# Two taps per matmul in the short convolution of the last 64 channels, plain loads on two issuing queues, and a new table of work

## The chip, the cores and the metric

The kernel runs on one core of a Trainium2 chip. The metric is the time of one execution on the device in microseconds (us); lower is better. TensorE (PE) multiplies matrices, VectorE (DVE), ScalarE (ACT) and GpSimd (POOL) do elementwise work, and SyncE (SP) does nothing but issue transfers. The transfers themselves (DMA) are moved by 16 DMA engines. Each of the five engines runs its own list of instructions in order.

## The reference

Two independent blocks are computed, and their outputs stand side by side in the last dimension (576 + 576 columns, 2048 rows, bf16).

Block A is an attention over four segments of 512 rows with 32 heads of 18 dimensions. Each segment has causal softmax attention of its own, plus a read of a memory that the earlier segments have summed up; a gate mixes the two, and a projection follows:

```python
for s in range(4):
    p = softmax(qs @ ks.T * scale + mask)           # 512 x 512 for each of 32 heads
    a_dot = p @ vs
    a_mem = (phi(qs) @ M) / (phi(qs) @ z + 1e-6)    # phi(t) = t+1 for t>0, else exp(t)
    outs.append(g * a_mem + (1 - g) * a_dot)
    M = M + phi(ks).T @ vs; z = z + phi(ks).sum(rows)
out_A = concat(outs) @ wo
```

Block B works on 576 channels of length 2048. The part that the change touches is the first line, a causal convolution with four taps for each channel:

```python
k_shift[s, c] = sum(shift_k[c, i] * k[s - i, c] for i in range(4))
kv = k_shift * v
y  = long_convolution(kv, ssm_k) + kv * ssm_D       # by a Fourier transform of length 4096
out_B = q * y
```

## The kernel before

The program is first recorded as a graph of about 1,600 small pieces of work (`Graph.add`), each with a name, the engines that may run it, and the tiles that it reads and writes. The order in which they are then written out is not decided by the code: it is a table, `ORDER`, of three characters for each piece (two for its number, one for its engine), and a second table, `PLACES`, says which copy of a tile each buffer gets. `place` reads both. So an engine's list of instructions follows the table, and a piece that has to wait holds up all that stands behind it in the same engine's list. Loads and stores are pieces too. In the kernel before all of them are on SP, and there are 225 of them. The semaphores of the DMAs go round eight places: each transfer waits at its issue until the transfer eight before it in the program has landed.

**Block A.** For each segment `s`, x is loaded transposed (`x{s}.{t}`, tiles `xT`), q and k are multiplied out in five groups of heads (`qk{s}.{m}`, tiles `dn`), written to a scratch in memory (`qd`, L861, `qk_scratch`) and read back padded to 32 rows a head (`pad`, L871). Four heads at a time (`i` from 0 to 31) the scores are computed (L1046), put through exp on ScalarE (`exs0_i`, `exs1_i`, `exs2_i`, L1053), masked on GpSimd (L1060) and multiplied with V (`av{i}`). The result goes by `ou` to a second scratch (`ad`, L1141, `a_scratch`), is read back in another layout (`am`, L1186, and the sums of the softmax as `cs`, L1156), normalised and mixed, and multiplied by `wo` (`out{s}.{tt}`, evacuated to one of two `oA` tiles by `eout`, stored by `oA{s}.{tt}`, L1255).

**Block B.** The channels are cut into groups of 128, 128, 128, 128 and 64. For each group k and v are loaded transposed, channels on partitions (`kT{ct}`, L374, and `vT{ct}`, L377, tiles `X4`, called `X` in the profile). The last group has only 64 new channels, and it loads the 128 channels from 448 on and uses the upper half. `conv` does the short convolution on TensorE: for each tap a diagonal 128 x 128 matrix of that tap's weights (`dg`, L388) times the transposed k, shifted by one column more for each tap, all four summed in PSUM. For each group there are four blocks of 512 columns, so 16 matmuls of 512 columns a group. `kv` (L404) multiplies by v. The rest of block B is a two-stage Fourier transform as matmuls (`F1`, `F2`), a product in frequency (`Q`, `P`, `Yi`, `Yr`), the way back (`inv`), a transposing transfer (`zt`, L566), a last stage and the product with q.

**Start of the program.** The tables of the transform are made on the chip: `w1idx` (DVE), `w1sin` (ACT, L258), `w1mask` (POOL), `psie` (POOL), and with these `psiT`, the first piece of work on TensorE; then four sines of 1024 columns (`sin`, L295) from index tiles that DVE makes (`idx`, L288 and L290). The loads at the start, in the order of SP's list: `wv`, five `x0` (L800), the rest of `wv`, `wk`, `beta1`, the rest of `wk`, the taps (`sk4`, L362, and `sk`, L357), `wq`, the first `kT0` and `vT0`, `Dt` (the 576 values of ssm_D as 4 partitions by 144, L350), the scratch's zeros.

Of the kernel before, what the change touches and what calls it, by code (L numbers as in the profile page):

```python
# [122 lines left out]
class Prog:  # L123
# [47 lines left out]
    def dma(self, name, fn, r, w, prio, nb, pk=1024, eng=16, issue=0.6, lat=1.5, al=()):  # L171
        per = {64: 0.009, 128: 0.012, 256: 0.018, 512: 0.028, 576: 0.030, 1024: 0.048, 1152: 0.052, 2048: 0.088, 4096: 0.160}
        k = min(per, key=lambda x: abs(x - pk))
        work = nb / pk * per[k] / eng
        return self.g.add(name, {"SP": issue}, fn, r=r, w=w, prio=prio, lat=lat, work=work * self.p["dmaw"], al=al)
# [52 lines left out]
    def build_b_front(self):  # L228
# [117 lines left out]
        def ld2(e):  # L346
            d = self.t(self.Dt)[:]
            dst = bass.AP(d.tensor, d.offset, [[32 * d.ap[0][0], 4], [1, 144]])
            src = bass.AP(self.B_D.tensor, self.B_D.offset, [[1, 4], [4, 144], [1, 1]])
            self.nc.sync.dma_start(out=dst, in_=src)  # L350

        g.add("Dt0", {"POOL": 0.3}, lambda e: self.nc.gpsimd.memset(self.t(self.Dt)[:, 0:144], 0.0), w=[self.Dt], prio=PT)
        self.dma("Dt", ld2, [], [self.Dt], p["prio_cl"], 1152, pk=64)

        def ld3(e):
            t = self.t(skb)
            self.nc.sync.dma_start(out=t[:, 0:4, :], in_=self.B_sk[0:512, :].rearrange("(t p) f -> p t f", p=P))  # L357
        self.dma("sk", ld3, [], [(skb, 0)], p["prio_cl"], 4096, pk=64)

        def ld4(e):  # L360
            t = self.t(skb)
            self.nc.sync.dma_start(out=t[:, 4, :], in_=self.B_sk[448:576, :])  # L362
        self.dma("sk4", ld4, [], [(skb, 1)], p["prio_cl"], 1024, pk=64)

    def conv(self, ct):
# [6 lines left out]

        def lk(e, kT=kT, c0=c0):
            self.nc.sync.dma_start_transpose(out=self.t(kT)[:, 16:16 + S], in_=self.B_k[0, :, c0:c0 + P])  # L374

# [3 lines left out]
        o = self.dma("kT%d" % ct, lk, [], [(kT, 1)], pr - p["lead_kt"], S * 256, pk=4096, issue=3.5, lat=1.8)  # L379
# [5 lines left out]
        def dgf(e, kT=kT, dg=dg, ct=ct):  # L385
            v = self.nc.vector if e == "DVE" else self.nc.gpsimd
            v.memset(self.t(kT)[:, 0:16], 0.0)
# [4 lines left out]
        for c in range(4):  # L392
            pc = Buf("ps1", "psconv")

            def cm(e, pc=pc, c=c, kT=kT, dg=dg):
                o = self.psf(pc)
                for i in range(4):
                    self.mm(o, self.t(dg)[:, i, :], self.t(kT)[:, 16 + 512 * c - i:16 + 512 * c - i + 512], i == 0, i == 3)
# [206 lines left out]
    def build_a_consts(self):  # L605
# [3 lines left out]
        for nm, src, lead in (("wq", "A_wq", 0), ("wk", "A_wk", 0.1), ("wv", "A_wv", 4), ("wo", "A_wo", 40)):  # L609
# [3 lines left out]
            if nm != "wo":  # L613
# [5 lines left out]
                def l1(e, b=b, src=src):  # L619
                    self.nc.sync.dma_start(out=self.t(b)[:, 0:4, :], in_=getattr(self, src)[0:512, :].rearrange("(t p) f -> p t f", p=P))  # L620

                def l2(e, b=b, src=src):
                    self.nc.sync.dma_start(out=self.t(b)[64:128, 4, :], in_=getattr(self, src)[512:576, :])

                self.dma(nm, l1, [], [(b, 0)], pr, 512 * 1152, pk=1152)
                self.dma(nm + "4", l2, [], [(b, 1)], pr, 64 * 1152, pk=1152)
            else:
                def l1(e, b=b):
                    self.nc.sync.dma_start(out=self.t(b)[0:126, 0:4, :], in_=self.A_wo[0:504, :].rearrange("(t p) f -> p t f", p=126))

                def l2(e, b=b):
                    self.nc.sync.dma_start(out=self.t(b)[0:72, 4, :], in_=self.A_wo[504:576, :])

                self.dma(nm, l1, [], [(b, 0)], pr, 504 * 1152, pk=1152)
                self.dma(nm + "4", l2, [], [(b, 1)], pr, 72 * 1152, pk=1152)
# [8 lines left out]
        def lb(e):  # L644
            src = bass.AP(self.A_beta.tensor, self.A_beta.offset, [[1, 32], [0, 4], [1, 1]])
            self.nc.sync.dma_start(out=self.t(bt)[:, 0:1], in_=src)

        self.dma("beta", lb, [], [(bt, 0)], p["prio_w"] + 20, 256, pk=64)

        for h in range(2):  # L650
            def lb2(e, h=h):
                src = bass.AP(self.A_beta.tensor, self.A_beta.offset + 16 * h, [[1, 16], [0, 8], [1, 1]])
                self.nc.sync.dma_start(out=self.t(bt)[:, 1 + h:2 + h], in_=src)

            self.dma("beta%d" % h, lb2, [], [(bt, 1 + h)], p["prio_w"] + 20, 256, pk=64)

        def lb3(e):
            src = bass.AP(self.A_beta.tensor, self.A_beta.offset + 28, [[0, P], [1, 4]])
            self.nc.sync.dma_start(out=self.t(bt)[:, 3:7], in_=src)

        self.dma("beta2", lb3, [], [(bt, 3)], p["prio_w"] + 20, 1024, pk=64)
# [80 lines left out]
        for j in range(4):  # L742
            def lw(e, j=j):
                self.nc.sync.dma_start(out=self.t(self.wop)[32 * j:32 * j + DH, :], in_=self.A_wo[504 + DH * j:504 + DH * j + DH, :])

            self.dma("wop%d" % j, lw, [(self.wop, "z")], [(self.wop, j)], self.tA(16), DH * 1152, pk=1152)
# [524 lines left out]
SHAPES = dict(A=([P, 4096], "bf16"), q=([P, 2048], "bf16"), xs=([P, 2048], "bf16"), X4=([P, 2064], "bf16"), H=([P, 1024], "bf16"), X=([P, 1024], "bf16"), T=([P, 1024], "bf16"), dg=([P, 4, P], "bf16"), xT=([P, L], "bf16"),  # L1271
# [14 lines left out]
    "0YG00G01D0oG02G0pD03D0cS0+S0-S11S10S0bG0qG06G04A05G0VG0RG0GG0HP07D08A0ID09D0BG0wG0zS0dS0ZS0iS0aS0US0XS0WS0TS1MG1RG0vG"  # L1286
    "0AA0CD0tSGoS0jSGpS0hS26P1wP22P14P18P1xA0DA19AGqD27D23D0ED1lD1CP12P1AP1kA13A1DD15D0FA1iGGrPGxPGvPGtP0rS0gSGWS1mD2BS0SS"
    "1BD0yS1YS0xSGyDGsDGwDGuD16P1nA0kA0PP0LP0NP17A1yP0QA0OAGzD1hA1zA0MDGXD1UP1VD0nG1oD1pDIiGH6PGaPGcPH4PGkPHAPG+PGdDGlDHCP"
    "GbAH7AHBAH5AHDAGiPGjD1XSIgS2CS0uSH2PGmPH0PH8PGYPGgPIOS1bSGnD1jD2AS1cSH1AG-A28P1NPH3A29AH9DGePHKPHXPI1PHIPHJDHLDGZAICS"
    "IDS1WS0sS1SP24PHYDGfAGhA1OA0lD20PI2A1TA25AHZPHxPHEPHkPHGPHTPHaAHyDH-PHzPHFDHlDI0AHHDHMD1GPH+AHNDI3D1PP1HAHUAIPD1qA1rD"  # L1290
    "HPG1KP1QA1LA1uD1sDHVPHWAI4DHbGI5DI6DHmPHOGHdGHnA1tA1EPHcG2QP1FA2RA1IP1+P2SA1-AIQPIWPISP21D1JDIXDIRAIUPIcPIePIdD0JPIVA"
    "IfAITAHoP0KD2XPHiPIaP2YA2ZAHpDHjDHQPIYP2IPIbD1vDIZDHRAHSA1ZS2KA2JAHeDHqDHrDHsDIpPIjPHtD2MP2NA2OA4cS4aS4bS4dS4ZS2PG2LG"
    "2aGJ6P4ePIhSJ7D5fP4fD5DD5gA2bP2dAJcP4iP2cA5CA4jA5IA2ES1eSKGS2DS4gP2TGIkDIqDJdD2qPHfP4hD5JD5EDHhD2UP2VDHgD1aS1dS4yS2WS"
    "0fSInPIoD2rA2sA59AKHD5KDJpP2iPJqA0mG5AG2jAIlP2kA4kP4lAKaG2eG2tG5GGImDIrD5BD2xPJrPHuPHwDHvD4mP2zA5FA2yAI7P4nAI8AI9DJsD"
    "5PGIwPIyPJNPJ0PIsPJ2PIxDJ4P5HDJ3DIuPIvDJ5D2lG2+GIzAItAJOAJ1AJ8P5OAJ9AJLP2fPI+P4oP5QD4pDI-AJCPJvPJtPJMA2gA2mPJDAJwAJuD"
    "JxDJyD5MD5dPIBS2FPIAS2GD2HD2oA2nAJeP2-P5eAIGP2pG2hSIIPIJDKYSJfA30A31A32GKUPJAPKMPKOPKSP64S65SIHDIKPJzGKPDKVAKNAKZS4+S"
    "KQPJPPKWPKIPJRPILDJBAJ+GKTAJSAJQDJgPJaPIEPKJDJbD5LA5NDIFDKRAKXA4sP4tA5RAJhD5SD5TDJEDJFDJTGJUDIMSJHDINS4zS1gSJWG4qP4rA"
    "2uP66S2vA33P34A3AP3BAJVG67SJGG2wS40S35S1fSK5S3wSK4SKbPKdP3CA5UAKcD5VDKeD5WD3EP3GAKfPKhP3FA3DG36P3HG37A38A39GKgDKiDKjD"
    "KKP4uPKLAJXP3LPLFP4vAJiGJjGJkGJYAJlGJZDLGDKwPKsPKqPKoP5bDKrD3NA3MAK+PKyP3IPKkPL0PKpDK-DKzDKlDKxAKtA5aA3JAL1A5cD4wP3PP"
    "4xD50S43S3KS3OGMSGKuPKvD54S51SJIP3QA3RAJKD3aPKmPJmP3xDKnD5YD3bA3cAJ-PL2PJoDJnAJJDL3AL4PLDP3WP3SG3yG5XAK1AL5D3TPK0D5ZD"  # L1300
    "K3S3UD3VSK2S3dGL6G46SMQSLJPLKD41P44P42D45D3YA3XA68S3ePLUPLEA3gA3fA3hGLVDL7DLjPLkD3ZG3lP3mA3nAL9G3oG5tP3pP5uDLWP3rA3qA"
    "3iPLYPLXD5vDLnPLoDLZA3sG6GP6HA6IA62P3jDLHPK8PLSPKAP63DLTA3tP3kSK9DKBD3uA6CP6DA52S6EALIA3vS5hP5wPMRS5lP5jPLaDLbD5nP5kA"
    "5iD5xD5oD5mAKCPK6P6JGLLG6KPKDD3zSK7DL8DLMD3+D0eS49S4CS5rP5pPMTP60P5qD61D53S6LA8dS8fS8hS8eS8gS5sA6MA3-G6RPMXPMUDMYDMZP"
    "47P6TA6SA6VPKFSM8SKES4-S6XA6WA6FG6UG55S6NGLdG6YG69P48DMaD6AD5+P4DPMVP6gP4ED5yP4AP6hA6iAMWD5-D4BD6BD5zD6OP6ZP6PA6cP4FP"
    "4KP8iP6aA6eA6dAMbD6jGLNG4MP4HP6bS58S6QS4LA8jA9GA6vP6xA6wA4IA6yG4GD4NDLlPMqP8oP9HD9IDMrD6fG8pD9KD9JALmA9LDA9SLzS9hP9iD"
    "M9D6kP8mP8nD8kP6lA6mA56S6rP4OS4JS8lDMAPMgPLhP6sAMBDLiDLOD6tA6nGMhAOCD9ED6uG8sP6oP8tA9DA6pDLAPLCD70PMMPMND8qP6zP8rDLBD"
    "71A72A9PA90S74PLPP4WP6+DLQD4XDLRD9FD76A75A6qS6-SOAS7qS7wS9jP9kDLcGLpGLqD57S73GLrD77GLsD78P79A7AA8uP7FP7HA7GA9QD8vD9RD"
    "8wP4PP7BG9NG91SA8S4QDMIPMkPMJD7JP4RP4UP8xAMlD7rD9WD4VD4SD7LA7KA7-S7IG7sG7MGMCP7CPMDA7DD7UP7xPMiP7WA7VA7zP7yD7+DLePMjD"
    "LgDLfAOBS9VA9MA7NP7QP95S96S7ES9XDABS80P82P8+P81D83D9TD8-DLtP7OA7RA7SALvDLuD9SAMKPMeP7YP9OD9cDMfD7ZA7aA7XG7TG7bG7PSLxS"
    "84SAASLwS8yPOJP7fPOFP9UD8zDOKD9fGOGDMLA7hA7gA9bAOHPOID7jP7iG7cP7lA7kA7mG9dD7dDMoPMGPMEPMmPMOP7eSMHAMPAMpDMnDMcPLySODP"  # L1310
    "MdAMFDAGP7nPOED7oDACS7pS89SO0S7tS8ES4YS92SN9P9pP9rP9nP9qDAHAAIANAA9oAAKPALA9sDOLD9tP87P9lP9eAAMA9uDM2PM4PNfPM5DMuPNKP"
    "MsPM0PNgANLAMvA9vP9mDM3D9gDM1D7uD9ZGAJGANG7vG8CPN5PL+PMwP9wA9YACkSChSClSCjSCiS9aDL-DM6S97S98S93SADPAEDMxAO1DMtAN6A9xP"
    "AOPAQAAPA85P8AP8HP9yD8FPMyP86D88D8BD8DD8GDNBPN7P9zGA0PA1DA2PARGMzANCAN8AASPAVPAXACmPCnAAWAA6PDWPCoPA3DATDDHACpA8ID4TS"
# [91 lines left out]
```

## Time and profile before

| what | value |
|---|---|
| median of three runs | 315.81 us (314.94 to 316.55) |
| the profiled execution's own time | 313.88 us, of which 312.2 us are the span of the instructions |
| mean granted TensorE clock | 0.956 |
| busy: PE, DVE, ACT, POOL | 272.5, 255.6, 249.9, 181.6 us |
| DMA: share of 16 engines over the span | 75.8 % |

The profile's busy times are those of instructions; the time of issuing a transfer isn't among them. A line such as `L374 SPq DMA_TRANSPOSE` is SP's queue issuing one. In a row of groups or of the timeline the bracket says how long the engine sat idle before it and what ended that. "DMA share" is the busy share of the 16 DMA engines in a stretch of time; it can pass 1, since the times of transfers that overlap on one engine are added. `xN` merges N instructions.

### The profile page before, as it was taken

The numbers are of one execution on the slowest core, as the hardware profiler recorded it, in microseconds if no ns is written. First come the engines' busy times: TensorE is split into PE (matmuls) and PEld (weight loads), VectorE is DVE, ScalarE is ACT, GpSimd is POOL, SyncE is SP. The second block draws the span as 40 slices with busy tenths as digits, with TensorE's granted clock in tenths as the row PEclk, the third lists the DMA queues.
The fourth block names the chain that finished last, engine by engine and source line by source line (L and its number), as shares of the span: only waits on it lengthen the run. The fifth ranks groups of instructions, "written<-read, shape, count | busy, mean of one in ns | idle before, by whom it ended". The sixth has DMA issues, their size and how long they took to land. (4 is left out here: it accounts for less than half of the span.)

```text
span 312.2 us, 8836 instructions
## 1 busy us (share of the span) xinstructions
PE 272.5 (87%) x3504; PEld 157.6 (50%) x3515; DVE 255.6 (82%) x460; ACT 249.9 (80%) x351; POOL 181.6 (58%) x229
## 2 busy tenths in 40 slices
PE   0599999899899989899987998989997987998695
PEld 0355776556654545455644556455663443543243
DVE  5598679999999999797998988988999857556851
ACT  2365879899999999679978987779998999799602
POOL 5798008399269996483764543946548665356200
PEclk9999999999999999999999999999997799589958
DMA  5788999985979798799979877759369478422401
GB/s 143 202 150 142 143 160 177 170 130 147 203 140 156 175 198 168 202 159 167 227 183 137 188 160 138 161 142 230 115 138 186 113 175 151 121 88 62 114 20 58
DMA packets 119011, 47.13 MB, mean 151 GB/s; under 512 B 101946, under 2 KB 112570, under 8 KB 118970
## 3 DMA queue, kind: packets, MB, share of 16 engines
q1 hardware_dynamic: 118970, 46.58, 75.8%
q8 instruction: 27, 0.44, 0.7%
q14 instruction: 14, 0.11, 0.1%
HBM read 17.74 MB, written 14.42 MB: 103 GB/s over the span
## 5 line engine op out<-in xcount | busy, mean ns | idle before, releaser
L1053 ACT ACTIVATE P<-PS 128x1024 bf16<-128x1024 f32 x160 | 154.2, 1035 | 20.2 <-PE PS L1046 16.1
L1060 POOL TENSOR_SCALAR_AFFINE_SELECT P<-P 128x512 bf16<-128x512 bf16 (+1 forms) x112 | 79.0, 724 | 64.7 <-ACT P L1053 46.1
L1046 PE MATMUL PS<-pad 18*128 18x256 bf16 (+3 forms) x512 | 41.9, 311 | 7.6 <-ACT P L1053 4.1
L158 DVE CAST A<-PS 128x512 bf16<-128x512 f32 (+1 forms) x62 | 40.2, 678 | 2.4 <-PE PS L152 2.2
L152 PEld LDWEIGHTS <-Ft 128*64 128x64 bf16 x704 | 23.3, 111 | 11.3 <-issue 7.3
L1046 PEld LDWEIGHTS <-pad 18*128 18x128 bf16 x512 | 12.2, 92 | 32.9 <-issue 28.5
L156 ACT CAST A<-PS 128x512 bf16<-128x512 f32 (+1 forms) x50 | 27.8, 623 | 1.3 <-PE PS L152 1.3
L150 PE MATMUL PS<-wo,am 126*128 126x288 bf16 (+1 forms) x152 | 27.7, 325 | 0.7 <-DVE am L1215 0.7
L534 POOL TENSOR_TENSOR H<-H 128x512 bf16<-128x512 bf16 x10 | 12.6, 1263 | 24.0 <-DVE H L524 24.0
L150 PE MATMUL PS<-xT,wq 128*126 128x512 bf16 (+1 forms) x100 | 25.5, 383 | 0.7 <-DMA xT<-in_A_x_dram 0.3
L150 PE MATMUL PS<-wv,xT 128*128 128x288 bf16 x160 | 25.1, 301 | 0.8 <-ACT P L1053 0.5
L152 PE MATMUL PS<-P,V 128*32 128x256 bf16 (+3 forms) x512 | 24.0, 315 | 1.6 <-POOL P L1060 0.4
L152 PE MATMUL PS<-W,xs 128*64 128x128 bf16 (+1 forms) x608 | 23.4, 218 | 2.4 <-DVE dn L158 0.8
L150 PE MATMUL PS<-xT,wk 128*126 128x512 bf16 (+1 forms) x100 | 25.4, 388 | 0.0
L152 PE MATMUL PS<-A,Ft 128*64 128x128 bf16 (+1 forms) x640 | 24.7, 216 | 0.7 <-ACT P L1053 0.2
L152 PEld LDWEIGHTS <-xs 128*64 128x64 bf16 (+1 forms) x608 | 19.0, 109 | 8.5 <-issue 7.6
L150 PEld LDWEIGHTS <-am 126*128 126x128 bf16 (+1 forms) x152 | 15.6, 109 | 11.1 <-issue 4.2
L150 PE MATMUL PS<-X,dg 128*128 128x512 bf16 x72 | 19.2, 380 | 1.6 <-DVE X L404 0.5
L152 PEld LDWEIGHTS <-V 128*32 128x32 bf16 x512 | 11.8, 99 | 16.3 <-issue 3.7
L150 PEld LDWEIGHTS <-xT 128*128 128x128 bf16 x160 | 15.4, 102 | 8.8 <-issue 3.3
L520 POOL TENSOR_TENSOR T<-X,H 128x512 bf16<-128x512 bf16 x14 | 17.8, 1291 | 2.4 <-ACT X L156 2.0
L158 DVE CAST oA<-PS 128x288 bf16<-128x288 f32 x20 | 9.0, 454 | 11.5 <-PE PS L150 9.7
(162 smaller groups left out, 538.7 us busy)
## 6 DMA issues: line engine op xcount, KB each, us to landing
pad<-qk_scratch SPq DMA_DIRECT2D x30, 256.0 KB
qk_scratch<-dn SPq DMA_DIRECT2D x16, 252.0 KB
a_scratch<-ou SPq DMA_DIRECT2D x31, 128.0 KB
out_dram<-oA SPq DMA_DIRECT2D x16, 144.0 KB
xs<-in_B_ssm_k_dram SPq DMA_DIRECT2D x4, 512.0 KB
q<-in_B_q_dram SPq DMA_DIRECT2D x8, 256.0 KB
out_dram<-q SPq DMA_DIRECT2D x8, 256.0 KB
am<-a_scratch SPq DMA_DIRECT2D x16, 126.0 KB
```

The lines of the kernel that those rows point to most:

```text
L150: self.nc.tensor.matmul(out, lhsT=lhsT, rhs=rhs, start=start, stop=stop)
L152: self.nc.tensor.matmul(out, lhsT=lhsT, rhs=rhs, start=start, stop=stop, tile_position=pos)
L156: self.nc.scalar.copy(out=out, in_=in_)
L158: self.nc.vector.tensor_copy(out=out, in_=in_)
L520: eng.tensor_tensor(out=t[:, 512 * r:512 * r + 512], in0=x[:, 512 * r:512 * r + 512], in1=h[:, 512 - 512 * r:1024 - 512 * r], op=ALU.mult)
L534: eng.tensor_tensor(out=t[:, 0:512], in0=t[:, 512:1024], in1=t[:, 0:512], op=ALU.subtract)
L1046: nc.tensor.matmul(o, lhsT=t[r, 1, q0:q0 + P], rhs=t[r, 0, q0:L], start=True, stop=True, tile_position=(32 * j, 0))
L1053: self.nc.scalar.activation(out=out2(jj), in_=self.psf(pso[jj]), func=ACT.Exp, scale=scale)
L1060: self.nc.gpsimd.affine_select(out=ap, in_=ap, compare_op=ALU.is_ge, fill=0.0, base=0, pattern=pat + [[1, P]], channel_multiplier=-1)
```

## The change

1. **Short convolution of the last group.** For `ct == 4` the tile of k now holds the 64 channels 512 to 575 twice: on partitions 64 to 127 as before from column 16 on, on partitions 0 to 63 shifted by one column. One matmul with a 128-row weight then does two taps, so two matmuls a block stand in place of four. The two halves are loaded by two calls of the transposing load, each of 64 channels (`kT4h1`, `kT4h0`, L382), where there was one of 128. The weights of the two taps are made by two small products, with three small memsets. Tile `X4` is 16 columns wider.
2. **Issuing queue.** Plain loads of weights, taps and gates may be issued by SP or ACT (`dq`, `two=True`). The table gives eleven of them to ACT: `wv` and its rest, the rest of `wk`, `wq`, three of the four `beta` loads, `sk`, `sk4` and two of `wop`. The other loads of that kind stay on SP. All stores and all transposing loads stay on SP.
3. **Table.** `ORDER` and `PLACES` are new throughout; pieces also change engine. The counts of pieces on DVE, ACT and POOL go from 400, 346 and 149 to 398, 352 (11 of them loads) and 156.

```diff
+    def dq(self, e):
+        return self.nc.scalar if e == "ACT" else self.nc.sync
+
...
-        return self.g.add(name, {"SP": issue}, fn, r=r, w=w, prio=prio, lat=lat, work=work * self.p["dmaw"], al=al)
+        return self.g.add(name, {"SP": issue, "ACT": issue} if two else {"SP": issue}, fn, r=r, w=w, prio=prio, lat=lat,
+                          work=work * self.p["dmaw"], al=al)
...
-            self.nc.sync.dma_start(out=t[:, 4, :], in_=self.B_sk[448:576, :])
-        self.dma("sk4", ld4, [], [(skb, 1)], p["prio_cl"], 1024, pk=64)
+            self.dq(e).dma_start(out=t[:, 4, :], in_=bass.AP(self.B_sk.tensor, self.B_sk.offset + 2048, [[0, 2], [4, 64], [1, 4]]))
+        self.dma("sk4", ld4, [], [(skb, 1)], p["prio_cl"], 1024, pk=64, two=True)
...
+        def lk2(e, kT=kT, h=0):
+            self.nc.sync.dma_start_transpose(out=self.t(kT)[64 * h:64 * h + 64, 17 - h:17 - h + S], in_=self.B_k[0, :, 512:576])
+
...
-        o = self.dma("kT%d" % ct, lk, [], [(kT, 1)], pr - p["lead_kt"], S * 256, pk=4096, issue=3.5, lat=1.8)
+        if ct < 4:
+            o = self.dma("kT%d" % ct, lk, [], [(kT, 1)], pr - p["lead_kt"], S * 256, pk=4096, issue=3.5, lat=1.8)
+        else:
+            for h in range(2):
+                o = self.dma("kT4h%d" % h, lambda e, h=h: lk2(e, h=h), [], [(kT, 1 + h)], pr - p["lead_kt"] - 0.1 + 0.1 * h, S * 128, pk=4096, issue=1.8, lat=1.8)
...
+            if ct == 4:
+                v.memset(self.t(kT)[0:64, 0:17], 0.0)
+                v.memset(self.t(kT)[64:P, 0:16], 0.0)
+                d = self.t(dg)
+                v.memset(d[:, 0:2, 0:64], 0.0)
+                for h in range(2):
+                    a = slice(64 * h, 64 * h + 64)
+                    v.tensor_tensor(out=d[a, 0:2, 64:P], in0=self.t(self.ident)[a, a].unsqueeze(1).to_broadcast([64, 2, 64]),
+                                    in1=self.t(self.skb)[a, 4, 1 - h:4 - h:2].unsqueeze(2).to_broadcast([64, 2, 64]), op=ALU.mult)
+                return
...
+                if ct == 4:
+                    for i in range(2):
+                        self.mm(o, self.t(dg)[:, i, :], self.t(kT)[:, 16 + 512 * c - 2 * i:16 + 512 * c - 2 * i + 512], i == 0, i == 1)
+                    return
...
-                    self.nc.sync.dma_start(out=self.t(b)[:, 0:4, :], in_=getattr(self, src)[0:512, :].rearrange("(t p) f -> p t f", p=P))
+                    self.dq(e).dma_start(out=self.t(b)[:, 0:4, :], in_=getattr(self, src)[0:512, :].rearrange("(t p) f -> p t f", p=P))
...
-                self.dma(nm, l1, [], [(b, 0)], pr, 512 * 1152, pk=1152)
+                self.dma(nm, l1, [], [(b, 0)], pr, 512 * 1152, pk=1152, two=True)
...
-SHAPES = dict(..., X4=([P, 2064], "bf16"), ...)
+SHAPES = dict(..., X4=([P, 2080], "bf16"), ...)
...
-ORDER = (...)
+ORDER = (...)
...
-PLACES = (...)
+PLACES = (...)
```

## The prediction

> **What bounds the kernel now.** The page first: the busy times, the slices and the queues; then windows of 8 us, where the work is even; then the timelines around the places that the diff touches.
>
> ```profile
> PE 272.5 (87%) x3504; PEld 157.6 (50%) x3515; DVE 255.6 (82%) x460; ACT 249.9 (80%) x351; POOL 181.6 (58%) x229
> ...
> PE   0599999899899989899987998989997987998695
> ...
> DMA  5788999985979798799979877759369478422401
> ...
> q1 hardware_dynamic: 118970, 46.58, 75.8%
> PE 3%; DMA 2%; DVE 1%; issue 0%; ACT 0%; DVEq 0%
> ```
>
> PE is the fullest engine, from 11 us on nearly without a gap, but DVE and ACT follow within 25 us, and the DMA engines are three quarters busy with some 119,000 packets. The chain that ended last goes back only into the last 24 us and names no engine for the rest. The windows say the same (PE, its weight loads, DVE, ACT, POOL; then the granted clock, the DMA share, GB/s):
>
> ```profile
> 24.00:32.00 8.00, 8.00 (x64) 4.43 (x62) 6.42 (x8) 4.43 (x8) 6.39 (x11) 1.00 0.81 154
> ...
> 144.00:152.00 8.00, 8.00 (x104) 4.58 (x102) 6.73 (x15) 7.64 (x12) 4.74 (x6) 1.00 1.13 185
> 152.00:160.00 8.00, 7.64 (x85) 4.11 (x80) 7.01 (x13) 7.14 (x9) 5.64 (x7) 1.00 1.04 233
> 160.00:168.00 8.00, 6.79 (x114) 4.10 (x112) 7.45 (x17) 6.40 (x9) 5.52 (x7) 1.00 0.74 120
> ```
>
> No engine has room for a long stop of its inputs. The last load of k stands in the third of these windows, in SP's list:
>
> ```profile
> 150.84 0.94 SPq L1255 DMA_DIRECT2D out_dram<-oA  x2
> 151.87 0.80 SPq L861 DMA_DIRECT2D qk_scratch<-dn  x1
> 152.78 2.90 SPq L1141 DMA_DIRECT2D a_scratch<-ou  x2
> 155.74 2.84 SPq L374 DMA_TRANSPOSE X<-in_B_k_dram  x1
> ```
>
> and DVE already waits there for a store to give a tile back:
>
> ```profile
> 156.78 0.46 DVE L158 CAST oA<-PS 128x288 bf16<-128x288 f32 x1 [0.85 <-DMA out_dram<-oA]
> ```
>
> **The change part by part.**
>
> *The two half loads (kT4h1, kT4h0).* The diff calls the transposing load for 64 channels. In the list of instructions of the changed kernel these two do not stand as `DMA_TRANSPOSE`, as every other load of k and v does, but as plain copies of 64 x 2048 x 1 elements: 64 partitions, 2048 rows, and between two rows a step of 1152 bytes in memory. Neighbours on a partition are not neighbours in memory, so each two-byte value is a piece of its own: 2 x 64 x 2048 = 262,144, over twice all the packets of the program now.
>
> One load of before has pieces of that size: `Dt`, L350, 576 values of two bytes. Alone in a window of 0.4 us (28.1 to 28.5) it shows:
>
> ```profile
> DMA packets 237, 0.00 MB, mean 1 GB/s; under 512 B 237, under 2 KB 237, under 8 KB 237
> ...
> q1 hardware_dynamic: 237, 0.00, 32.7%
> ```
>
> 0.4 us x 16 engines x 0.327 = 2.09 us for 237 packets, 8.8 ns of one engine each. Spread over 16 engines: 262,144 x 8.8 ns / 16 = 144 us. That is my price.
>
> Bounds. The table load `xs<-in_B_ssm_k` has 128-byte packets, in 23.5 to 24.5:
>
> ```profile
> DMA packets 1674, 0.21 MB, mean 214 GB/s; under 512 B 1674, under 2 KB 1674, under 8 KB 1674
> ...
> q1 hardware_dynamic: 1674, 0.21, 140.2%
> ```
>
> 1674 a microsecond give 157 us. Its share of 1.40 shows packets overlapping on an engine; if two-byte ones did so too, 144 / 1.40 = 103 us. If making the descriptors were the limit, not moving them: its 4096 packets took 5.2 us from issue on, 788 a microsecond, 333 us; and Dt ran at 237 / 0.4 = 593, 442 us, though it used only four engines. The moving price stands, since while xsh's packets flow the engines are never idle.
>
> What waits. All stores, all reads back from the scratches and all transposing loads are on SP's queue, and they are behind the copies. In before, Dt is issued at 25.71 and moves at 28.1, after xsh's packets: the queue works in order. Besides, each transfer waits at its issue until the one eight before it has landed, so SP itself stops eight transfers on. In the new table the halves stand with the first exponentials of head group 10, 146.45 in before, and issue at about 147 to 150. Behind them: a store of `oA` right away, which the next `eout` of DVE (L158) needs, and this cast stands just before the exponentials of group 12 (156.93 in before). `cs` and `am` (L1156, L1186) of the segment come too late as well, so PE stops at `num1.0`, and `pad`, so the scores stop. I take 10 us of slack between the copies' start and DVE's stop: 134 us of the 144 show. Behind the stopped DVE stand its evacuations of PSUM, so PE and ACT stop with it. Starting again costs the store and the read back, 2.55 + 2.30 us by the rows at the end of before, less what DVE has to do meanwhile: +4 (0 to 10; PE also shows half its clock after idling there).
>
> A rule of the Trainium skill bears on this: "DMA: Bandwidth & Descriptors", section "Rules for kernel authors", has transposes done by the hardware's transpose, not by a plain copy with a rearranged access pattern, and gives a 19-fold difference. Taken on the 2.84 us above, an estimate, that is 54 us for the whole 128 channels' worth, and the sum would be about 363; the two-byte row of this trace says 144, and I go by the row.
>
> *Two taps per matmul.* Eight of 80 matmuls of 512 columns go (80 weight loads of `dg` are recorded, of the matmuls 72). Seven took 1.68 us in the row below, 0.24 each, so -1.9. PE is near full where they are (175 to 181). What is added, three memsets and two small products, is under 1 us on POOL or DVE, beside work that waits for the copies anyway; POOL (58%) covers it, and without that cover it would cost its 1 us.
>
> ```profile
> 21.28 1.68 PE L150 MATMUL PS<-X,dg 128*128 128x512 bf16 x7
> ```
>
> *Loads from ACT's queue at the start.* In before the sine for the first table comes early:
>
> ```profile
> 6.22 1.28 ACT L258 ACT_TABLE_LOAD   x1 [6.22 <-DVE xs L253]
> 7.52 0.42 ACT L258 ACTIVATE W<-xs 128x256 bf16<-128x256 int32 x1
> ...
> 9.26 1.11 POOL L615 MEMSET wq<- 64x576 bf16 x1
> ...
> 11.14 0.40 PE L150 MATMUL PS<-ident,Pe 32*128 32x32 bf16 x2 [11.14 <-POOL Pe L310]
> ```
>
> In the new list seven loads stand ahead of it on ACT (wv, two beta, sk4, the rests of wv and wk, sk), each about 0.6 us of issue, and some wait at issue for the transfer eight before: wk's rest for the fourth x load, which landed at 7.97 in before. So the table load starts at about 8.6, the sine's matrix is there at 10.3 instead of 7.94, +2.4. The memset of wq (1.11) no longer stands in the chain on POOL: PE starts at 12.4 instead of 11.14, +1.2 (0 to +2.4). From 12 to 32 PE is full, so this goes through. SP has eleven issues fewer, some 6 us, but no first matmul of PE waited for those; wq and wk come on time from either queue: 0, at most -1. The ACT table is loaded twice instead of four times, -2.6 us of ACT, under PE's bound: 0.
>
> *The table.* By the rows, DVE gets 1.5 us less, ACT 2.5 less and 6 more of issue, POOL 11 more. PE has 25 us of idle in all that a better order could take, and a worse one double. Tail order is the same but for a few places. 0, with +-4.
>
> **Sum.** 313.9 (the profiled execution, 1.9 under the median) + 144 - 10 + 4 - 1.9 + 1.2 = 451.2. On the median's scale 453.
>
> **Rivals.**
>
> *Quicker copies, 405 to 435.* Either packets overlap as the 128-byte ones do: 103 instead of 144, 412. Or later transfers overtake them, and only the last `conv` waits, at 175 instead of 157: -18, 435. For: shares above 1 in the windows around. Against: Dt waited its turn.
>
> *Slower copies.* Two-byte pieces limited by descriptor making: 333 us gives 641, 442 gives 750; between moving price and that, 475 to 600, if the other half of the stall is other queues' small writes competing. For: Dt's engines were only partly busy in its window. Against: it went to four engines of 16.
>
> *The other side: not slower.* The copies stay hidden, at the place where they are issued. The point: 262,144 values in the 10 us of slack, 26,000 a microsecond, 0.6 ns of an engine each, as if neighbouring rows' or channels' values were gathered into long pieces (64 channels of one row do lie together in memory, 128 bytes). Then the head and the matmuls remain: 313.9 + 1.2 - 1.9 = 313.2, 315.1 on the median's scale. Against: no two-byte packet took under 7 ns in this trace, and the instruction lists the row as its inner dimension. A gathered form would also show as `DMA_TRANSPOSE`.
>
> **How the numbers follow.** The likeliest: 45%, its own range 435 to 475 (8.2 to 10 ns a value, restart and table). Quicker, 405 to 435: 20%. Slower, 475 to 600: 17%; above 600: 11%. Not slower: 4%. Between 320 and 405, a gathering of some values: 3%. The range 405 to 600 holds 82%. A measurement of this kernel can tell some 0.5% (1.6 us): of the 4% I give 2 to faster, 2 to the same; all else is slower.
>
> **What would show it.** In the changed kernel's profile: two `DMA_DIRECT2D` of `in_B_k` at L382 beside four `DMA_TRANSPOSE` at L374; some 381,000 packets; a gap of about 130 us from about 157 with all four engines idle, DMA engines busy at a few GB/s, and at its end DVE's `oA` waiting for `out_dram<-oA`. If SP's later transfers land inside the gap, the order of the queue was wrong; if the gap is far longer with idle DMA engines, descriptor making; if there is no gap, the reading of the copies as two-byte pieces. 72 weight loads of dg and first work on PE at about 12.4 check the small terms, and two table loads on ACT. The forecast is wrong above all if a two-byte piece among 262,144 costs something else than among 576.

## The result: 651.1 us against 315.4

The changed kernel takes 651.07 us (median of four runs, 643.85 to 658.58) against 315.38 (313.74 to 316.55): a ratio of 2.049, interval 2.029 to 2.070. Every ratio here and below compares the faster executions of each kernel alone (here 643.85 and 648.37 us of the changed one), so it is not the quotient of the two medians. The profiled execution is the longest of the four, 658.58 us, of which 656.5 are its span. Its page:

```profile
span 656.5 us, 8823 instructions
PE 268.3 (41%) x3498; PEld 157.5 (24%) x3507; DVE 258.8 (39%) x457; ACT 245.8 (37%) x344; POOL 190.6 (29%) x240
...
PE   1999988898500000000000000000000789988886
...
PEclk9899997999855555555555555555555799999988
DMA  6958798769999999999999999999999998865731
...
DMA packets 379092, 47.13 MB, mean 72 GB/s; under 512 B 362028, under 2 KB 372652, under 8 KB 379052
...
q1 hardware_dynamic: 376692, 45.20, 135.1%
q10 hardware_dynamic: 2360, 1.38, 0.8%
```

The busy times of the engines are nearly those of before; the span has doubled around them. Half of the slices hold a stop in which PE does nothing and its granted clock falls to half. In the same slices the DMA engines are full, and 260,081 more packets stand in the program's account than before (379,092 against 119,011), though the bytes are the same 47.13 MB. `q10` is ScalarE's queue.

The stop in windows (PE, its weight loads, DVE, ACT, POOL; clock, DMA share, GB/s), and SP's list of issues through it:

```profile
160.00:165.00 5.00, 5.00 (x80) 3.10 (x80) 4.30 (x10) 4.61 (x7) 4.78 (x6) 1.00 0.94 168
165.00:200.00 35.00, 8.94 (x107) 5.08 (x102) 7.54 (x15) 7.41 (x10) 7.68 (x9) 0.65 1.93 3
200.00:300.00 100.00, 0.00 (x0) 0.00 (x0) 0.00 (x0) 0.00 (x0) 0.00 (x0) 0.50 1.95 1
350.00:450.00 100.00, 0.00 (x0) 0.00 (x0) 0.00 (x0) 1.36 (x2) 0.00 (x0) 0.50 1.95 2
510.00:520.00 10.00, 7.12 (x92) 3.86 (x91) 4.88 (x11) 4.75 (x6) 2.83 (x4) 0.66 0.84 177
```

```profile
161.86 1.16 SPq L382 DMA_DIRECT2D X<-in_B_k_dram  x1
163.12 179.96 SPq L1010 DMA_TRANSPOSE phk<-fk  x1
343.18 0.66 SPq L382 DMA_DIRECT2D X<-in_B_k_dram  x1
343.94 163.47 SPq L1281 DMA_DIRECT2D out_dram<-oA  x2
507.50 0.91 SPq L1167 DMA_DIRECT2D a_scratch<-ou  x2
```

The two half loads are the `DMA_DIRECT2D` at L382. Behind each of them the very next transfer is stuck in its issue until the copy is nearly through: 179.96 us behind the first and 163 of the 163.47 us behind the second, where the row merges two stores. And DVE waits as the prediction said, for a store to give back the `oA` tile, where it waited 0.85 us before:

```profile
173.12 0.45 DVE L158 CAST V<-PS 128x288 bf16<-128x288 f32 x1
512.13 0.82 DVE L158 CAST oA<-PS 128x288 bf16<-128x288 f32 x2 [338.56 <-DMA out_dram<-oA]
```

338.6 of the 344.7 us between the two profiled executions (658.58 - 313.88) are this one wait. What was predicted for it was 138 (144 - 10 + 4). The packets of a stretch of each copy, 200 to 300 and 400 to 500, in two answers of the DMA view:

```profile
DMA packets 72175, 0.14 MB, mean 1 GB/s; under 512 B 72175, under 2 KB 72175, under 8 KB 72175
...
q1 hardware_dynamic: 72175, 0.14, 195.4%
```

```profile
DMA packets 79792, 0.16 MB, mean 2 GB/s; under 512 B 79792, under 2 KB 79792, under 8 KB 79792
...
q1 hardware_dynamic: 79792, 0.16, 194.9%
```

That is 722 and 798 pieces a microsecond. At a share of 1.95 a piece takes 16 x 100 x 1.954 / 72,175 = 43 ns of an engine in the first copy and 39 ns in the second, and by that share two pieces overlap on an engine nearly all the time; the prediction's row gave 8.8.

### The profile page after: what moved, and what is told of

It is laid out like the page before. It is cut to its first block, busy times and chain, and to the rows that moved or that the text cites. A ratio compares the mean times of both kernels' runs of the same rounds, so it can differ in the third digit from the quotient of the medians.

```text
span 656.5 us, 8823 instructions
## 1 busy us (share of the span) xinstructions
PE 268.3 (41%) x3498; PEld 157.5 (24%) x3507; DVE 258.8 (39%) x457; ACT 245.8 (37%) x344; POOL 190.6 (29%) x240
## 2 busy tenths in 40 slices
DMA packets 379092, 47.13 MB, mean 72 GB/s; under 512 B 362028, under 2 KB 372652, under 8 KB 379052
## 5 line engine op out<-in xcount | busy, mean ns | idle before, releaser
L150 PE MATMUL PS<-wo,am 126*128 126x288 bf16 (+1 forms) x152 | 26.1, 311 | 340.8 <-DVE oA L158 338.7
L158 DVE CAST oA<-PS 128x288 bf16<-128x288 f32 x21 | 9.4, 454 | 347.6 <-DMA out_dram<-oA 338.6
L1198 POOL TENSOR_TENSOR xf<-rb,m 128x512 bf16<-128x512 bf16 x5 | 5.2, 1039 | 349.0 <-PE PS L152 341.9
L150 PEld LDWEIGHTS <-am 126*128 126x128 bf16 (+1 forms) x152 | 14.9, 104 | 349.0 <-issue 344.4
L915 ACT ACTIVATE fk<-dn 126x512 bf16<-126x512 bf16 (+1 forms) x15 | 9.6, 639 | 176.8 <-DMA phk<-fk 176.4
L1072 PE MATMUL PS<-pad 18*128 18x384 bf16 (+3 forms) x512 | 40.8, 307 | 9.0 <-ACT P L1079 2.9
L150 PE MATMUL PS<-xT,wq 128*126 128x512 bf16 (+1 forms) x100 | 27.3, 407 | 1.2 <-DMA xT<-in_A_x_dram 0.3
L560 POOL TENSOR_TENSOR H<-H 128x512 bf16<-128x512 bf16 x15 | 17.8, 1188 | 22.8 <-DVE H L550 19.5
L158 DVE CAST dn<-PS 126x512 bf16<-126x512 f32 (+1 forms) x27 | 18.3, 682 | 7.6 <-PE PS L150 7.1
```

The costliest lines, as they stand in the source:

```text
L150: self.nc.tensor.matmul(out, lhsT=lhsT, rhs=rhs, start=start, stop=stop)
L158: self.nc.vector.tensor_copy(out=out, in_=in_)
L560: eng.tensor_tensor(out=t[:, 0:512], in0=t[:, 512:1024], in1=t[:, 0:512], op=ALU.subtract)
L915: self.nc.scalar.activation(out=self.t(ff)[0:M], in_=self.t(dense[m])[0:M, w_, :], func=ACT.Exp)
L1072: nc.tensor.matmul(o, lhsT=t[r, 1, q0:q0 + P], rhs=t[r, 0, q0:L], start=True, stop=True, tile_position=(32 * j, 0))
L1198: eng.tensor_tensor(out=self.t(xf)[sl].rearrange("p (c x) -> p c x", c=8), in0=self.t(rb)[sl, 0:64].unsqueeze(1).to_broadcast([n, 8, 64]), ...
```

## The experiments

### The copies, taken out and put in

`one_load` keeps all of the change but the way k of the last group comes:

```diff
+            if h == 0:
+                return
-            self.nc.sync.dma_start_transpose(out=self.t(kT)[64 * h:64 * h + 64, 17 - h:17 - h + S], in_=self.B_k[0, :, 512:576])
+            self.nc.sync.dma_start_transpose(out=self.t(kT)[:, 16:16 + S], in_=self.B_k[0, :, 448:576])
```

The two-tap weights and matmuls of the last group are taken out with it, so that it uses four taps like the others.

> The changed kernel with its new table and its loads from ScalarE's queue, but k of the last group loaded by one transposing load of 128 channels and convolved with four taps, as before. Theory: the two plain copies are the whole loss (DVE's one wait in the changed kernel is 338.6 us), and what is left is the later start of TensorE, 14.13 us against 11.14: 315.4 + 3 = 318 us (314 to 322). Rival: the new table and queues save something that the copies hide, below 313. Second rival: the new table itself is worse by more than its start, above 323.

Measured: 321.10 us (319.07 to 321.74), ratio 1.018 (1.012 to 1.024), within the theory's 314 to 322. The copies, with what hangs on them, are 330 of the 336 us lost. What stays, 5.9 us, is about twice what the later start of PE, 14.04 us against 11.14, would explain.

`before_halves` is the opposite: the old table, all loads on SP, and only the two calls for 64 channels.

```diff
+            if ct == 4:
+                for h in (1, 0):
+                    self.nc.sync.dma_start_transpose(out=self.t(kT)[64 * h:64 * h + 64, 17 - h:17 - h + S], in_=self.B_k[0, :, 512:576])
+                return
             self.nc.sync.dma_start_transpose(out=self.t(kT)[:, 16:16 + S], in_=self.B_k[0, :, c0:c0 + P])
```

> The kernel before with its own table and all loads on SP; only the last group's k is loaded by the two calls for 64 channels, with the two-tap weights and matmuls. Theory: the copies cost the same wherever they stand, 262,144 pieces at 730 to 800 a microsecond = 328 to 359 us of which some 10 are hidden; 315.4 + 340 = 655 (630 to 675). Rival: the new table puts them in a bad place and the old one hides more: below 600.

Measured: 646.16 us (one run), as the theory had it (630 to 675). The copies cost the same in the old table. SP's list in this kernel shows the second copy stuck behind the first, and `cs` behind the second:

```profile
158.72 164.81 SPq L376 DMA_DIRECT2D X<-in_B_k_dram  x2
323.64 164.17 SPq L1174 DMA_DIRECT2D cs<-a_scratch  x1
```

So the loss is that of the copies, in either table. Both went at 798 a microsecond here; why the first one in the changed kernel ran at 722 was not tried.

### What a piece costs

`pieces` is a kernel of loads. Those into the tile `T` wait for one another, since they write the same place; the transposing load and the last one go to another tile, so each of them runs beside a load into `T`:

```diff
+    strided = src([[1, 64], [576, 512], [1, 1]])
+    nc.sync.dma_start(out=T[0:64, 0:512], in_=strided)
+    nc.sync.dma_start(out=T[0:64, 0:512], in_=src([[1024, 64], [2, 512], [1, 1]]))
+    nc.sync.dma_start(out=T[0:64, 0:1024].rearrange("p (n t) -> p n t", t=2), in_=src([[2, 64], [576, 512], [1, 2]]))
+    nc.sync.dma_start(out=T[0:64, 0:64], in_=src([[1, 64], [576, 64], [1, 1]]))
+    nc.sync.dma_start(out=T[0:64, 0:8192].rearrange("p (n t) -> p n t", t=64), in_=src([[2304, 64], [576, 128], [1, 64]]))
+    nc.sync.dma_start_transpose(out=T2[:, 16:16 + 2048], in_=B_k[0, :, 448:576])
+    nc.sync.dma_start(out=T[0:64, 0:512], in_=strided)
+    nc.scalar.dma_start(out=T2[0:64, 0:512], in_=strided)
```

> Only loads, one after another (nothing of the reference is computed, the output is zeros): 64 x 512 values of two bytes 1152 bytes apart (a quarter of a half); as many values 4 bytes apart; as many pieces of four bytes, 1152 apart; 64 x 64 values; 64 x 128 pieces of 128 bytes; the transposing load of 128 channels; and at the end the first load on SP's and on ScalarE's queue at once. Theory 1, pieces of any kind are made at some 750 a microsecond: 44, 44, 44, 5.5, 11 us; two queues at once 44 us if each makes its own, 88 if they share. Theory 2, reads far apart in memory are what is slow, and near ones go at the 8.8 ns an engine of the row that the prediction used: 44, 18, 44, 5.5, and 5 us (1674 a microsecond) for the 128-byte pieces. Theory 3, the price falls with few pieces: 64 x 64 in 2.3 us, the big ones 44.

Measured, from its list of issues (these five are issued when the one before has landed):

```profile
7.68 0.72 SPq L48 DMA_DIRECT2D T<-in_B_k_dram  x1
52.01 0.55 SPq L50 DMA_DIRECT2D T<-in_B_k_dram  x1
104.02 0.60 SPq L52 DMA_DIRECT2D T<-in_B_k_dram  x1
125.19 0.60 SPq L54 DMA_DIRECT2D T<-in_B_k_dram  x1
132.29 0.60 SPq L56 DMA_DIRECT2D T<-in_B_k_dram  x1
```

Two bytes far apart took 44.3 us, two bytes near each other 52.0 (stores of zeros ran beside both), four bytes far apart 21.2. So it is not the distance (theory 2 falls), and it is not the making of pieces, of which there were as many in the third load (theory 1 falls in that form). The 8,192 pieces of 128 bytes took 10.4 us, beside the transposing load; theory 1 had 11 and theory 2 five, so for pieces of that size this run leaves theory 1 standing. On both queues at once, 150 to 200 us:

```profile
DMA packets 38549, 0.08 MB, mean 2 GB/s; under 512 B 38549, under 2 KB 38549, under 8 KB 38549
...
q10 hardware_dynamic: 19276, 0.04, 97.6%
q1 hardware_dynamic: 19273, 0.04, 97.6%
```

That is 771 a microsecond for both together: each queue gets half, and what limits lies behind them. This agrees with the Trainium skill, "DMA: Bandwidth & Descriptors", section "Issuing engines are not separate DMA queues", by which transfers of all issuing engines run on the same 16 and interleave.

The load of 64 x 64 values, 127.0 to 127.5 us, holds the prediction's mistake:

```profile
DMA packets 1139, 0.00 MB, mean 5 GB/s; under 512 B 1139, under 2 KB 1139, under 8 KB 1139
...
q1 hardware_dynamic: 1139, 0.00, 127.2%
```

0.5 x 16 x 1.272 / 1139 = 8.9 ns a piece, the 8.8 of `Dt`. All 4,096 pass between 126.5 and 129 us. But in the last half microsecond of the same load a piece already took 21 ns (485 packets, 127.0 %), and in the long load it is 39. In a load of 16,384 pieces, the second one of `pieces2` below, both can be seen, 39 to 40 us and 42 to 43:

```profile
DMA packets 1462, 0.00 MB, mean 3 GB/s; under 512 B 1462, under 2 KB 1462, under 8 KB 1462
...
q1 hardware_dynamic: 1462, 0.00, 80.8%
```

```profile
DMA packets 739, 0.00 MB, mean 1 GB/s; under 512 B 739, under 2 KB 739, under 8 KB 739
...
q1 hardware_dynamic: 739, 0.00, 193.3%
```

8.8 ns a piece and then 42. The first few thousand are quick and the rest are not: theory 3, and a load of 576 values never gets that far. What makes the start quick was not tried.

`pieces2` asks what about two bytes is slow, 16,384 pieces a load:

```diff
+    nc.sync.dma_start(out=T[0:64, 0:256], in_=src([[1, 64], [576, 256], [1, 1]]))
+    nc.sync.dma_start(out=gap(T, 256, 32), in_=src([[1, 64], [576, 256], [1, 1]]))
+    nc.sync.dma_start(out=gap(T, 256, 32, 2), in_=src([[2, 64], [576, 256], [1, 2]]))
+    nc.sync.dma_start(out=gap(T[:, 1:], 256, 32, 2), in_=src([[2, 64], [576, 256], [1, 2]]))
+    nc.sync.dma_start(out=gap(T, 256, 32, 16), in_=src([[2, 64], [576, 256], [1, 16]]))
+    nc.sync.dma_start(out=gap(T, 256, 32), in_=src([[1, 64], [0, 256], [1, 1]]))
+    nc.sync.dma_start(out=gap(T, 256, 32), in_=T2[0:64, 0:2048].rearrange("p (n t) -> p n t", t=8)[:, :, 0:1])
+    nc.sync.dma_start(out=sc[0:64, :].rearrange("p (n t) -> p n t", t=32)[:, :, 0:1], in_=gap(T, 256, 32))
```

> Only loads again (output zeros, nothing of the reference computed), 64 x 256 = 16,384 pieces each, one after another: two bytes side by side on the partition; two bytes 64 bytes apart on the partition; four bytes 64 apart; four bytes from an odd value on; 32 bytes; two bytes all from one place in memory; two bytes out of the chip's own memory; two bytes written to memory. After some 4,000 pieces that go faster, the pieces of two bytes went at 798 a microsecond and those of four at 1700. Theory 1, a write of less than four bytes is slow: all of the two-byte loads into the chip's memory take some 20 us, wherever they come from and land, four bytes and 32 bytes some 10; four bytes from an odd value on 20. Theory 2, writes beside each other hold each other up: 64 bytes apart falls to 10 us. Theory 3, the reading is slow: the load out of the chip's own memory and the one from one place fall to 10 us or less.

```profile
14.51 0.72 SPq L51 DMA_DIRECT2D T<-in_B_k_dram  x1
37.18 0.59 SPq L53 DMA_DIRECT2D T<-in_B_k_dram  x1
61.26 0.60 SPq L55 DMA_DIRECT2D T<-in_B_k_dram  x1
73.03 0.60 SPq L57 DMA_DIRECT2D T<-in_B_k_dram  x1
97.26 0.59 SPq L59 DMA_DIRECT2D T<-in_B_k_dram  x1
109.17 0.60 SPq L61 DMA_DIRECT2D T<-in_B_k_dram  x1
265.13 0.63 SPq L63 DMA_DIRECT2D T<-T  x1
289.00 0.55 SPq L65 DMA_DIRECT2D sc<-T  x1
320.66 0.49 SPq L66 DMA_DIRECT2D T<-sc  x1
```

In the order of the diff: 22.7, 24.1, 11.8, 24.2, 11.9, 156.0, 23.9 and 31.7 us (the last issue is a small load that closes the list). Two bytes side by side and 64 bytes apart cost the same (theory 2 falls), two bytes out of the chip's own memory cost the same as from outside (theory 3 falls for what is read). Four bytes and 32 bytes cost half, but four bytes that begin at an odd value cost as much as two. Past the quick start the gap is wider: 739 pieces a microsecond for two bytes (42 to 43 us), 1,700 for four (68 to 69). What the loads of 23 to 24 us share is that a written piece does not cover whole four-byte words: theory 1. Longer pieces from an odd value on were not tried, and how the chip does such a write is not shown by these runs. No theory had a price for two bytes written to memory, 31.7 us. The 156 us of the load that reads one place over and over was foreseen by none either, and theory 1's 20 us fail there; the engines were mostly idle in it (a share of 0.05).

`pieces3` writes 65,536 values on 64, 128, 64 and 32 partitions:

```diff
+    nc.sync.dma_start(out=T[0:64, 0:1024], in_=src([[1, 64], [576, 1024], [1, 1]]))
+    nc.sync.dma_start(out=T[:, 0:512], in_=src([[1, 128], [576, 512], [1, 1]]))
+    nc.sync.dma_start(out=T[64:128, 0:1024], in_=src([[1, 64], [576, 1024], [1, 1]]))
+    nc.sync.dma_start(out=T[64:96, 0:2048], in_=src([[1, 32], [576, 2048], [1, 1]]))
```

> Only loads of 65,536 single values, 1152 bytes apart, one after another (output zeros, nothing of the reference computed): on partitions 0 to 63, on all 128, on 64 to 127, on 64 to 95. Theory 1, the limit is one for the whole core, 722 to 798 a microsecond: all four take 82 to 91 us. Theory 2, it goes by the partitions written (the useless copy on 128 partitions ran at 1234 a microsecond): 82, 53, 91, and over 150 us. In both the first 4,000 or so go at over 1500 a microsecond, which is the price that the prediction took from 576 values.

```profile
4.27 0.76 SPq L46 DMA_DIRECT2D T<-in_B_k_dram  x1
90.00 0.65 SPq L48 DMA_DIRECT2D T<-in_B_k_dram  x1
145.99 0.63 SPq L50 DMA_DIRECT2D T<-in_B_k_dram  x1
230.86 0.66 SPq L52 DMA_DIRECT2D T<-in_B_k_dram  x1
```

The first three took 85.7, 56.0 and 84.9 us, and the last one about as long (the copy that waits for it starts at 315.64). Neither theory is right as it stood: 128 partitions go 1.5 times as fast as 64, but 32 go no slower than 64. The limit is not proportional to the partitions.

### Does another queue help?

Both kernels are `one_load` with a useless copy of 36,864 single values where the second half copy stood, from one queue or the other:

```diff
             if h == 0:
+                self.nc.scalar.dma_start(out=self.tiles["junk"][:], in_=bass.AP(self.B_k.tensor, self.B_k.offset + 448, [[1, P], [D, 288], [1, 1]]))
                 return
```

> The same useless copy of 36,864 single values, from SP's queue at the same place. Theory: 46 us of copy less the 5 to 10 us by which the stores behind it may be late: 357 to 362, and the wait for the oA tile some 38 us. If the price of few pieces held, 8.8 ns an engine as in the prediction, 20 us of copy: 331 to 336.

> The kernel with one load and four taps, and beside it, where the second half copy stood, a useless plain copy of 128 x 288 single values (36,864 pieces, 46 us at 798 a microsecond) from ScalarE's queue into a tile of its own. Theory: the order of SP's queue is what stops the kernel, so on another queue SP's transfers pass it and share the engines, until the transfer eight further has to wait for the same semaphore place: 335 to 350 (321 + 46 less the time of eight transfers and more). Rival: the 16 engines are full of two-byte pieces and nothing passes: as in SP's queue, 321 + 46 - 5 = 362.

Measured: 351.38 us from SP's queue, 351.63 from ScalarE's (one run each). None of the four ranges was met. From SP's, the price was smaller than expected, some 30 us over `one_load`, since the copy has 128 partitions: 12,338 pieces in 10 us (180 to 190), where 798 a microsecond had been reckoned. DVE waited 26.0 us for `out_dram<-oA`. From ScalarE's queue SP's next seven transfers did pass, and then the same loss came by another way, SP's own wait (columns: waiting, for what, us in total, times, longest):

```profile
SPq L1171 <- DMA junk<-in_B_k_dram: 23.5, 1, 23.5
```

That is the semaphore place that the copy holds: the eighth transfer after it, `cs`, waits at its issue until the copy has landed. So the order of SP's queue is not the only thing that stops the kernel, and in this program moving such a copy to the other queue did not save it.

### The rest: queue, table, two taps

`one_load_sp` puts all plain loads of the new table back on SP; `before_act` gives the old table's eleven to ScalarE:

```diff
+        if o.eng == "ACT" and "SP" in o.engs:
+            o.eng = "SP"
...
+        if o.name in ("wv", "wv4", "wk4", "wq", "beta0", "beta1", "beta2", "sk", "sk4", "wop0", "wop3"):
+            o.eng = "ACT"
```

> The new table with one load and four taps and all plain loads on SP, each at its place in the new table. Theory: the table carries the loss, 319 to 322, as with ScalarE's queue. Rival: the queue carries it, and the time falls to 316 or less.

> The kernel before with its own table, but the eleven loads that the new table gives to ScalarE are issued from ScalarE's queue, each at its place in the old table. Theory: the 6 us by which the new table and queues are slower are the table's, and the queue is worth little: 314 to 317. Rival: the queue is the loss (loads that wait at issue hold up the sine and the table's other work): 318 to 321.

Measured: new table on SP 317.47 us (314.26 to 320.76) beside 317.42 before, ratio 1.000 (0.995 to 1.005); old table with ScalarE's loads 320.05 (317.01 to 321.86), ratio 1.013 (1.005 to 1.022). Before itself took 2 us more on this chip than beside `one_load` (315.18), so 317.47 lies between the two ranges that were set, and the ratios decide: the rival holds in both, the queue is the loss and the table is none. In the old table the effect is small: the two medians alone, 320.05 and 317.42, are 0.8 % apart. With the new table's loads back on SP, PE starts early:

```profile
9.96 0.40 PE L152 MATMUL PS<-ident,Pe 32*128 32x32 bf16 x2 [9.96 <-POOL Pe L316]
```

In the old table with ScalarE's loads, PE starts at 11.14 as before and then stands, and ACT stands too:

```profile
15.77 2.80 PE L152 MATMUL PS<-wv,xT 128*128 128x288 bf16 x11 [2.80 <-DMA wv<-in_A_wv_dram]
```

```profile
9.89 0.53 ACTq L628 DMA_DIRECT2D wv<-in_A_wv_dram  x1
...
16.58 1.06 ACT L300 ACTIVATE Ft<-xs 128x1024 bf16<-128x1024 int32 x1 [5.63 <-DMA Dt<-in_B_shift_k_dram]
```

The rest of `wv` is issued at 9.89 instead of 7.83, behind a sine, and the second of the four large sines comes at 16.58 instead of 13.28, behind loads that wait. A list shared by loads and arithmetic makes each late for the other.

`sine_first` tries to mend the head by order: five loads after the sine.

```diff
+    late = [out[at[n]] for n in ("beta1", "sk4", "wv4", "wk4", "sk")]
+    i = at["w1sin"]
+    out[:i + 1] = [o for o in out[:i + 1] if o not in late] + late
```

> The kernel with one load and four taps and the new table; of ScalarE's first instructions only wv and one load of beta stay ahead of the sine, the five other loads (beta, sk4, the rests of wv and wk, sk) come after it. Theory: the head's 3 us come from the sine standing behind loads that wait at issue; TensorE starts at 11.2 to 11.5 instead of 14.0 and the kernel takes 318 to 319 instead of 321.1. Rival: wv's rest now comes too late for TensorE's first work on V, and nothing is won: 321 or more.

Measured: 323.63 us, ratio 1.021 (1.013 to 1.029). PE starts at 9.95 and after its first matmuls stands 2.26 us, until 13.68, for the rest of `wv`: the rival, nothing won.

```profile
13.68 2.80 PE L154 MATMUL PS<-wv,xT 128*128 128x288 bf16 x11 [2.26 <-DMA wv<-in_A_wv_dram]
```

So an early start of PE is worth nothing by itself, if what it needs next comes late.

`shift` (new table) and `before_shift` (old one) have two taps per matmul without the copies of single values. k of the last group comes by one load of 128 channels as in `one_load`, and a copy makes the other half (of both edits only that copy is printed):

```diff
+            if ct == 4:
+                self.nc.sync.dma_start(out=self.t(kT)[0:64, 16:16 + S], in_=self.t(kT)[64:P, 15:15 + S])
             self.nc.sync.dma_start_transpose(out=self.t(vT)[:, 0:S], in_=self.B_v[0, :, c0:c0 + P])
```

> The changed kernel, two taps per matmul kept, but the tile is filled another way: one transposing load of 128 channels, and then, just before the last load of v, a plain copy inside SBUF of the upper 64 partitions to the lower 64, one column further (64 pieces of 4096 bytes). Theory: eight matmuls fewer, 1.9 us less than the kernel with one load and four taps, so about 316. Rival: the copy must wait for the transposing load and stands in SP's queue, or the place of the matmuls has slack, and nothing is gained: within 1 us of one load and four taps, or above it.

> The kernel before, with its table and all loads on SP; the last group's k comes by one transposing load of 128 channels, a plain copy inside SBUF ahead of the last load of v makes the half that is one column further, and two taps go in one matmul. Theory: eight matmuls of 0.24 us fewer where TensorE is near full, 313.3 against 315.2 (0.994). Rival: as in the kernel with the new table, where this brought nothing (322.3 against 321.1): 315 to 317, since SP's queue gains a transfer that waits and TensorE is not what sets the end there.

Measured: 322.3 us, 1.024 (1.018 to 1.031), where the same kernel with four taps had 1.018 (the rival holds); and 318.13, 1.011 (1.005 to 1.017) in the old table, above what theory and rival had. The eight matmuls are gone (72 weight loads of `dg`, 80 before), the time is not. These kernels pay a transfer of 256 KB more on SP's list, so they show that this way of doing it does not pay, not what the matmuls alone are worth.

## Why the prediction was wrong

The step that failed is the price of one piece: "0.4 us x 16 engines x 0.327 = 2.09 us for 237 packets, 8.8 ns of one engine each", and from it 144 us. The copies took 344 (from the first two-byte packets at about 164 to 508.4), 21 ns of elapsed time an engine. The 8.8 follows from the row, and the load of 64 x 64 gives 8.9 again; but it is the price of the first few thousand pieces, and what was to be priced were 262,144. The prediction named this itself as its weak point and gave it no bound of its own. The rest of that path was right: 344.4 less 9.5 us before DVE stops and plus 3.7 to start again is the measured wait of 338.6, where 144 - 10 + 4 was said.

The bounds did not hold it either: the range ended at 600. The overlap of packets on an engine, which was to make the copies quicker (103 us), is there, at a share of 1.95, and each piece takes the longer for it. Of the terms outside, 333 us from 788 packets a microsecond comes out near the measured 344, but that is luck, for its reason fell: it took making descriptors to be the limit, and four-byte pieces from the same queue went at 21,606 in 12 us, 1,800 a microsecond (108 to 120 in `pieces`). The engines were not idle in the stop, as that rival had them; they were full.

Point by point:

- That the calls for 64 channels are plain copies of single values: right. 260,081 packets more than before; 262,144 said.
- Where the stop begins: at DVE's `oA` cast, right, some 9.5 us after the first two-byte packets; 10 said.
- Starting again: DVE goes on 3.7 us after the copies' end; 4 said, and the clock is at 0.66 in the 10 us window there.
- That SP stops eight transfers on: wrong for SP's own queue, where the very next issue is stuck for 180 and 163 us; right for a copy on the other queue.
- "Dt waited its turn", later transfers don't overtake: right in outcome, but hardly tested, since the next issue on SP was itself stuck. The time said for `Dt` is off: 98 of its packets moved from 27 to 28 us, before the 28.1 of the prediction, though still after xsh's.
- Two taps, -1.9: there are 72 weight loads as said, but no kernel here shows a gain from it.
- The head, +1.2: PE started at 14.13, not 12.4, so +3.0. The sine's table load came at 9.73 instead of 8.6, and the sine's matrix with it, at 11.44 instead of 10.3. All of the loads on ScalarE's queue cost 1.3 % in the old table (`before_act`) and, by the difference of two ratios taken on two chips, 1.8 % in the new; the bound of +2.4 was too low. Where the part beyond the head's 3 us goes was not settled.
- The table, 0 with +-4: right, 1.000 with loads on SP.
- The table loads on ACT, two instead of four: right; what that alone is worth was not tried.

The prediction weighed a rule of the Trainium skill against the row ("DMA: Bandwidth & Descriptors", section "Rules for kernel authors": 19-fold) and got a sum of 363, further off than the row's. It took the 19 on 2.84 us, which is the time that SP needs to issue the transposing load, not the time until that load has landed. In `pieces` the transposing load of 128 channels took 11.5 us from issue to landing, beside another load, against 344 us for the two half copies of 64: some 30-fold at the least. So the trace agrees with the rule's advice, and the rule's figure is the smaller one.

## What to carry to other kernels

Look at what a transposing call became in the built program: with 64 channels instead of 128 it was a plain copy of single values, though the source still calls a transposing load. Price many pieces by a row with many pieces: a short transfer shows the quick start, not the steady rate, and two-byte pieces here settled at 722 to 798 a microsecond on 64 partitions, under half the 1,700 of four-byte ones. A load given to an engine that also computes is late when the arithmetic waits and makes the arithmetic late when the load waits.

## What the runs showed that was not expected

- 16,384 written pieces that do not cover whole four-byte words cost double: 24.1 us for two bytes and 24.2 for four bytes from an odd value on, 11.8 for four bytes on their place and 11.9 for 32.
- 128 partitions take single values 1.5 times as fast as 64 (56.0 us for 65,536 against 85.7), and 32 no slower than 64.
- A load that reads the same value of memory 256 times a partition took 156 us for 16,384 pieces, 105 a microsecond.
- A long copy held the next issue on its own queue for nearly its whole length (179.96 us), and one on the other queue held the eighth transfer after it, for 23.5 us, by the shared round of eight semaphores.
